# A decode block on one core: a head's wq and wo in two loads at two places of the turn instead of one

## The chip, the cores and the metric

The kernel runs on one core of one Trainium2 chip. The metric is the device time of one execution, in microseconds (us); lower is better. Three runs of the kernel before gave 1358.25 to 1359.9 us, median 1359.09. All data is float32.

## The reference, cut to what matters

One new token for each of B = 2 sequences goes through an attention block with a cache and then through a bilinear feed-forward block:

```python
q = (_layernorm(x) @ wq).reshape(B, 1, 16, 256)           # D = 448 -> 16 heads of 256
scores = einsum("bhqd,bhkd->bhqk", q, k_cache) * 256**-0.5 # 8192 keys per head and sequence
o = einsum("bhqk,bhkd->bhqd", softmax(scores), v_cache)
h = x + o.reshape(B, 1, 4096) @ wo
n = _layernorm(h)
h2 = h + ((n @ w_gate) * (n @ w_up)) @ w_down
```

`k_cache` and `v_cache` hold 2 x 16 x 8192 x 256 numbers each. All of both caches must be read once, together with the weights: 561 MB by the profile's count.

## The kernel before, in words

**Tiling.** One head and one sequence ("a query", b = 0 or 1) has 8192 keys. They come in NCH = 2 chunks of 4096 keys, each a tile of 128 partitions x 32 keys x 256 numbers, 4096 KB. There are two K buffers (`k_sb[0]`, `k_sb[1]`) and two V buffers (`v_sb[0]`, `v_sb[1]`), one for each chunk number. A load may start into a buffer only when the engine that reads its old contents is through with them.

**Engines.** VectorE (DVE) does the scores: for each half chunk a product (L222, `prod`) and a reduction (L225, `s_sb`), so four instructions for a chunk. TensorE (PE) mixes V with the softmax weights (`mix`, L252), projects the next head's query (`query`, L206 and L211, from `wq_sb`) and adds the head's part of the output projection (`mixed`, L270, from `wo_sb`). ScalarE (ACT) does the exponentials and small copies. SyncE (SP) issues every load, strictly in the order of the program: a load that has to wait holds up all loads behind it.

**The loop.** `For_i` over the 16 heads (L428) has three arms: the first head, the last head with the feed-forward behind it, and the fourteen heads between, all through `query_steps`. A turn works on b = 0 and then on b = 1 of its head. V runs one query behind K: while K of (head h, b = 0) is scored, V of (head h - 1, b = 1) is loaded and mixed, and with K of (h, 1) goes V of (h, 0). So `wo` of head h - 1 is first needed in the b = 0 part of turn h (L270, `if b == B - 1` of the previous query), and `wq` of head h + 1 in the b = 1 part of turn h, between the mixing of the two chunks of V (L295 to L298).

**The order of the loads.** A turn of the middle arm issues nine loads. In this text a and b stand for the turn's first and second query:

| load | K0a | V0a | W | K1a | V1a | K0b | V0b | K1b | V1b |
|---|---|---|---|---|---|---|---|---|---|
| KB | 4096 | 4096 | 896 | 4096 | 4096 | 4096 | 4096 | 4096 | 4096 |
| completion semaphore | 0 | 1 | 2 | 3 | 4 | 5 | 6 | 7 | 0 |

W is one load into the tile `w_sb`, whose first half is `wo` of head h - 1 and whose second half is `wq` of head h + 1 (L175, called at L284).

**The waits.** The framework that builds the program writes all waits itself. Its rule, read from the compiled program of the kernel before: every load adds to one of eight completion semaphores, given out in turn, 0 to 7 and then 0 again, starting at 0 in each arm; and a load is issued only when all earlier loads on its own semaphore have landed, those of the previous turn included. K0a, the first load of a turn, waits in that program for semaphore 0 (so for V1b of the turn before, the last load on it), for semaphore 5 (K0b of the turn before, which wrote the same buffer) and for DVE's last product on `k_sb[0]`. V0a waits for semaphores 1, 6 and 7 and for PE's `mix` of `v_sb[0]`. W waits for semaphore 2 and for PE's last `query` matmul of the turn before. V1a waits for semaphore 4 and for PE's whole previous turn. The first arm issues three loads in the loop, the last arm twenty-one, on the same eight semaphores from 0 on.

Of the kernel before, what the change touches and what calls it, by code (L numbers as in the profile page):

```python
# [8 lines left out]
F32 = mybir.dt.float32  # L9
# [4 lines left out]
B, D, H, SK, DH, F = 2, 448, 16, 8192, 256, 1792  # L14
EPS = 1e-5
P = 128
# [9 lines left out]
WQ, WO = 3 * DH + DH // 2, 2 * D  # L26
# [17 lines left out]
def tile_decode_block(  # L44
# [2 lines left out]
    x: bass.AP,  # L47
    k_cache: bass.AP,
    v_cache: bass.AP,
    w: bass.AP,  # L50
    wg: bass.AP,
    wu: bass.AP,
    wd: bass.AP,
# [12 lines left out]
    nc = tc.nc  # L66
    ctx.enter_context(tc.manual_schedule())
    const = ctx.enter_context(tc.tile_pool(name="const", bufs=1))
# [35 lines left out]

    k_sb = [const.tile([P, JC, DH], F32, name=f"k_sb{c}") for c in range(NCH)]
    v_sb = [const.tile([P, JC, DH], F32, name=f"v_sb{c}") for c in range(NCH)]
    w_sb = const.tile([P, WO + WQ], F32, name="w_sb")
    wo_sb, wq_sb = w_sb[:, :WO], w_sb[:, WO:]
    ff_sb = const.tile([P, NF * D], F32, name="ff_sb")
    q_sb = [const.tile([P, DH], F32, name=f"q_sb{b}") for b in range(B)]  # L110
    s_sb = [const.tile([P, NJ], F32, name=f"s_sb{b}") for b in range(B)]
# [52 lines left out]
    def load_cache(dst, src, bh, c, parts=(JC,)):  # L164
        n = P * JC
        keys = src.rearrange("b h s d -> (b h) s d")[bass.ds(bh, 1), c * n : (c + 1) * n]
        keys = keys.rearrange("o (p j) d -> p (o j) d", p=P)
        at = 0
        for k in parts:
            nc.sync.dma_start(dst[:, at : at + k, :], keys[:, at : at + k, :])  # L170
            at += k

    def load_w(h, lo=0, hi=WO + WQ):

        nc.sync.dma_start(w_sb[:, lo:hi], w[bass.ds(h, 1)].rearrange("o p n -> p (o n)")[:, lo:hi])  # L175

    load_w(H - 1, lo=WO)

    nc.vector.tensor_copy(x_sb[:, D:], x_sb[:, D - HALF : D])
    xT = transposed(x_sb, "x")  # L180
# [22 lines left out]
    def query(b):  # L203

        for c in range(DC - 1):
            nc.tensor.matmul(  # L206
                q_ps[b][:, :DH], xb[:, c, b, :], wq_sb[:, c * DH : (c + 1) * DH],
                start=(c == 0), stop=False,
            )
        for k in range(2):  # L210
            nc.tensor.matmul(  # L211
                q_ps[b][:, k * HD : (k + 1) * HD], xb[:, DC - 1 + k, b, :], wq_sb[:, 3 * DH :],
                start=False, stop=(k == 1),
            )

    def take_query(b):
        nc.scalar.activation(q_sb[b], q_ps[b][:, :DH], AF.Copy)  # L217

    def scores(b, part, at=k_sb):

        c, k = divmod(part, 2)
        nc.vector.tensor_mul(  # L222
            prod, at[c][:, k * HC : (k + 1) * HC, :], q_sb[b][:, None, :].to_broadcast([P, HC, DH])
        )
        nc.vector.tensor_reduce(  # L225
            s_sb[b][:, part * HC : (part + 1) * HC], prod, axis=AX.X, op=ALU.add
        )

    def top(b):

        nc.vector.tensor_reduce(m_sb, s_sb[b], axis=AX.X, op=ALU.max)  # L231
        nc.tensor.transpose(sm_ps[0][:1, :P], m_sb, ident)  # L232

    def softmax(b):
        nc.vector.tensor_reduce(nm_sb, sm_ps[0][:1, :P], axis=AX.X, op=ALU.max, negate=True)  # L235
        nb_ps = sm_ps[1][:, 0:1]
        nc.tensor.matmul(nb_ps, row, nm_sb, start=True, stop=True)  # L237
        nc.scalar.activation(nb_sb, nb_ps, AF.Copy)  # L238
        nc.scalar.activation(  # L239
            p_sb[b], s_sb[b], AF.Exp, bias=nb_sb, scale=DH**-0.5, accum_out=lsum_sb  # L240
        )
        nc.tensor.matmul(sm_ps[1][:, 1:2], ones, lsum_sb, start=True, stop=True)  # L242

    def norm():
        nc.vector.reciprocal(rl_sb, sm_ps[1][:, 1:2])

    def mix(b, c):

        for t in range(c * JC // 2, (c + 1) * JC // 2):
            j = 2 * t - c * JC  # L250
            g = 32 * (t % 4)
            nc.tensor.matmul(  # L252
                o_ps[b][g : g + 2, :], p_sb[b][:, 2 * t : 2 * t + 2], v_sb[c][:, j : j + 2, :],
                start=(t < 4), stop=(t >= NJ // 2 - 4),
            )

    def mixed(b, last=False):

        nc.scalar.activation(o_sb, o_ps[b], AF.Copy)  # L259
        oT_ps = sm_ps[1][:, 2:4]  # L260
        for c in range(2):
            for k in range(2):
                nc.tensor.matmul(  # L263
                    oT_ps[:, c : c + 1], o_sb[:, (2 * k + c) * P : (2 * k + c + 1) * P],
                    sel[:, k : k + 1], start=(k == 0), stop=(k == 1),
                )
        nc.scalar.activation(oT_sb[:, :, b], oT_ps, AF.Copy, scale=rl_sb)  # L267
        if b == B - 1:
            for c in range(2):
                nc.tensor.matmul(  # L270
                    acc_ps, oT_sb[:, c, :], wo_sb[:, c * D : (c + 1) * D],
                    start=False, stop=(last and c == 1),
                )

    def query_steps(h, first, more):

        for b in range(B):
            before = b > 0 or not first
            for c in range(NCH):
                if not first or (b > 0 and c > 0):  # L280
                    load_cache(k_sb[c], k_cache, b * H + h, c)
                    load_cache(v_sb[c], v_cache, h if b else H - 1 + h, c)
                if c == 0 and b == first:
                    load_w(h, WO if first else 0, WO + (WQ if more else 0))  # L284
            at = k_sb if before else k_first
            scores(b, 0, at)
            if before:
                softmax(1 - b)
            scores(b, 1, at)
            if before:  # L290
                norm()
            for part in range(2, 2 * NCH):
                scores(b, part, at)
            for c in range(NCH):
                if c > 0 and b == 1 and more:  # L295
                    query(0)
                    query(1)
                    take_query(0)  # L298
                if before:
                    mix(1 - b, c)  # L300
            if before:
                mixed(1 - b)
            top(b)
            if b == 1 and more:
                take_query(1)
# [8 lines left out]
    def attend_last():  # L314

        for c in range(NCH):
            load_cache(v_sb[c], v_cache, B * H - 1, c, LAST if c == NCH - 1 else (JC,))
        load_w(0, hi=WO)
        nc.sync.dma_start(wg_t, wg)
        softmax(1)  # L320
        norm()
        mix(1, 0)
        nc.sync.dma_start(wu_t, wu)
        mix(1, 1)

        at = 0
        for n in (8, 4, 2):
            nc.sync.dma_start(
                wd_t[:, at : at + n, :].rearrange("p n d -> p (n d)"), wd[:, at * D : (at + n) * D]
            )  # L330
            at += n
        mixed(1, last=True)
# [113 lines left out]
def pack(np, inputs):  # L446

    got = {n: np.ascontiguousarray(inputs[n]) for n in ("A_x", "A_k_cache", "A_v_cache")}
    wq, wo = np.asarray(inputs["A_wq"]), np.asarray(inputs["A_wo"])
    rows = []  # L450
    for h in range(H):
        a = wq[:, h * DH : (h + 1) * DH]
        top = a[: 3 * P].reshape(3, P, DH).transpose(1, 0, 2).reshape(P, 3 * DH)
        last = np.concatenate([a[3 * P :, :HD], a[3 * P :, HD:]], axis=0)
        rows.append(np.concatenate([top, last], axis=1))

    wo = wo.reshape(H, 2, P, D).transpose(0, 2, 1, 3).reshape(H, P, WO)
    got["w"] = np.concatenate([np.roll(wo, 1, axis=0), np.roll(np.stack(rows), -1, axis=0)], axis=2)
    for name in ("B_w_gate", "B_w_up"):
        a = np.asarray(inputs[name])  # L460
        top = a[: 3 * P].reshape(3, P, F).transpose(1, 0, 2).reshape(P, 3 * F)
        col = [a[3 * P :, FO[g] : FO[g] + FG[g]] for g in range(4)]
        last = np.concatenate(
            [np.concatenate([col[k], col[k + 2]], axis=1) for k in range(2)], axis=0
        )
        got[name] = np.concatenate([top, last], axis=1)
    a = np.asarray(inputs["B_w_down"]).reshape(NF, P, D)
    a = a[[FO[g] // P + n for n, g in FF]]
    got["wd"] = a.transpose(1, 0, 2).reshape(P, NF * D)
    return {k: np.ascontiguousarray(v) for k, v in got.items()}  # L470
# [25 lines left out]
```

## Time and profile before

| what | us |
|---|---|
| median of 3 runs | 1359.09 |
| the profiled execution: device time | 1357.73 |
| its span in the profile | 1355.9 |
| DVE busy | 1153.7 |
| PE busy | 554.5 |
| time in which DMA packets were under way, as a share of 16 engines' span (SP's queue) | 96.9% |

The profile page gives each engine's busy time, the mean DMA rate and the chain of work that ended last. Other views answer for a window of time: the timeline of one engine in order (start, duration, instruction, what it waited for), the busy times and the DMA rate of a stretch, the chain of work piece by piece, SP's own waits, and for a load the time from issue to landing. The times in these views count from the span's start, so the 1.8 us between the span and the device time lie around the span.

### The profile page before, as it was taken

How to read it: one execution, taken by the hardware profiler on the slowest of the kernel's cores; microseconds unless marked ns; L12 is line 12 of the kernel's file. 1: busy time of each engine (PE TensorE's matmuls, PEld its weight loads, DVE VectorE, ACT ScalarE, POOL GpSimd, SP SyncE). 2: the span in 40 equal slices, each digit the busy share in tenths (PEclk: the TensorE clock that was granted, in tenths of full speed). 3: DMA queues.
4: the chain of work that ended last, by engine and by line, in shares of the span. 5: the costliest groups of instructions: out<-in, count | busy, mean ns of one | idle time of the engine just before them, and what ended most of it. 6: DMA issues, size and time to landing. Idle time of an engine off the chain costs nothing.

```text
span 1355.9 us, 9160 instructions
## 1 busy us (share of the span) xinstructions
PE 554.5 (41%) x3094; PEld 194.1 (14%) x3094; DVE 1153.7 (85%) x395; ACT 61.7 (5%) x197; POOL 1.2 (0%) x8
## 2 busy tenths in 40 slices
PE   3224455252352633524334453434425245263347
PEld 2111111020020210201111021111102002021013
DVE  7999989798897988889898897988979889898871
ACT  1000000000000000000000000000000000000000
POOL 0000000000000000000000000000000000000000
PEclk7567766676775656768667566677767666576668
DMA  9999898999999999999999999999999999999998
GB/s 409 408 426 433 372 437 372 441 430 389 433 397 432 432 392 431 395 430 433 393 430 394 429 402 428 433 388 431 400 429 433 397 433 388 429 433 400 433 422 342
DMA packets 22213, 561.45 MB, mean 414 GB/s; under 512 B 2482, under 2 KB 2484, under 8 KB 5044
## 3 DMA queue, kind: packets, MB, share of 16 engines
q1 hardware_dynamic: 22184, 561.20, 96.9%
q8 instruction: 13, 0.21, 0.1%
q14 instruction: 4, 0.03, 0.0%
q10 hardware_dynamic: 12, 0.01, 0.0%
HBM read 561.19 MB, written 0.00 MB: 414 GB/s over the span
## 4 chain that ended last, share of the span: by engine, by line
DMA 59%; DVE 36%; PE 3%; issue 2%; DVEq 0%; ACT 0%; SPq 0%; ACTq 0%
DMA k_sb<-in_A_k_cache_dram 59%; DVE prod L222 23%; DVE s_sb L225 12%; PE o_ps L252 1%; PE q_ps L352 1%; PE sm_ps L156 0%; PE y_ps L411 0%; PE acc_ps L270 0%; PE q_ps L206 0%; DMA x_sb<-in_A_x_dram 0%; DVEq L222 0%; PE acc_ps L198 0%; PE sm_ps L135 0%; PE sm_ps L263 0%; SPq L170 0%
## 5 line engine op out<-in xcount | busy, mean ns | idle before, releaser
L222 DVE TENSOR_TENSOR prod<-k_sb,q_sb 128x4096 f32<-128x4096 f32 x126 | 556.9, 4420 | 156.0 <-DMA k_sb<-in_A_k_cache_dram 147.8
L225 DVE TENSOR_REDUCE s_sb<-prod 128x16 f32<-128x4096 f32 x128 | 565.8, 4420 | 5.4
L252 PE MATMUL o_ps<-v_sb,p_sb 128*2 128x512 f32 x2048 | 357.6, 862 | 335.0 <-DMA v_sb<-in_A_v_cache_dram 227.3
L237 PE MATMUL sm_ps<-nm_sb,row 1*128 1x1 f32 x64 | 17.9, 347 | 325.7 <-DVE nm_sb L235 312.5
L252 PEld LDWEIGHTS o_ps<-v_sb,p_sb 128*2 128x2 f32 x2048 | 58.6, 107 | 592.2 <-issue 457.5
L237 PEld LDWEIGHTS sm_ps<-nm_sb,row 1*128 1x128 f32 x64 | 15.7, 302 | 332.8 <-issue 197.8
L206 PE MATMUL q_ps<-w_sb,xb 128*128 128x256 f32 x192 | 50.2, 399 | 0.0
L259 ACT ACTIVATE o_sb<-o_ps 128x512 f32<-128x512 f32 x32 | 19.1, 597 | 641.3 <-PE o_ps L252 641.3
L263 PE MATMUL sm_ps<-sel,o_sb 128*128 128x1 f32 x256 | 33.7, 253 | 25.7 <-ACT o_sb L259 25.7
L270 PE MATMUL acc_ps<-w_sb,oT_sb 128*2 128x448 f32 x64 | 38.2, 736 | 5.6 <-ACT oT_sb L267 5.6
L232 PE MATMUL sm_ps<-ident,m_sb 128*1 128x128 f32 x32 | 10.1, 314 | 73.2 <-DVE m_sb L231 73.2
L263 PEld LDWEIGHTS sm_ps<-sel,o_sb 128*128 128x128 f32 x256 | 31.0, 191 | 56.4 <-ACT o_sb L259 56.4
L206 PEld LDWEIGHTS q_ps<-w_sb,xb 128*128 128x128 f32 x192 | 35.1, 197 | 18.6 <-issue 14.9
L242 PE MATMUL sm_ps<-lsum_sb,ones 128*128 128x1 f32 x64 | 18.7, 361 | 25.3 <-ACT p_sb L239 25.3
L238 ACT ACTIVATE nb_sb<-sm_ps 128x1 f32<-128x1 f32 x32 | 5.5, 171 | 449.8 <-PE sm_ps L237 449.8
L211 PEld LDWEIGHTS q_ps<-w_sb,xb 128*128 128x128 f32 x128 | 19.8, 196 | 1.8
L242 PEld LDWEIGHTS sm_ps<-lsum_sb,ones 128*128 128x128 f32 x64 | 16.0, 309 | 28.1 <-ACT p_sb L239 28.1
L211 PE MATMUL q_ps<-w_sb,xb 128*128 128x128 f32 x128 | 19.9, 279 | 0.0
L217 ACT ACTIVATE q_sb<-q_ps 128x256 f32<-128x256 f32 x32 | 12.2, 380 | 134.7 <-PE q_ps L211 129.1
L232 PEld LDWEIGHTS sm_ps<-ident,m_sb 128*1 128x1 f32 x32 | 2.5, 79 | 92.1 <-issue 60.0
L362 DVE COPY h_sb<-acc_ps 2x448 f32<-2x448 f32 x1 | 0.6, 612 | 14.4 <-PE acc_ps L270 14.4
L239 ACT ACTIVATE p_sb<-s_sb,nb_sb 128x64 f32<-128x64 f32 x32 | 11.1, 348 | 1.0
(78 smaller groups left out, 95.7 us busy)
## 6 DMA issues: line engine op xcount, KB each, us to landing
v_sb<-in_A_v_cache_dram SPq DMA_DIRECT2D x63, 4096.0 KB, 32.7
k_sb<-in_A_k_cache_dram SPq DMA_DIRECT2D x62, 4096.0 KB, 25.3
w_sb<-in_w_dram SPq DMA_DIRECT2D x14, 896.0 KB, 22.7
k_sb<-in_A_k_cache_dram SPq DMA_DIRECT2D x2, 2048.0 KB, 10.0
v_sb<-in_A_k_cache_dram SPq DMA_DIRECT2D x1, 4096.0 KB, 20.9
ff_sb<-in_B_w_gate_dram SPq DMA_DIRECT2D x1, 3136.0 KB, 22.2
v_sb<-in_B_w_up_dram SPq DMA_DIRECT2D x1, 3136.0 KB, 18.5
v_sb<-in_A_v_cache_dram SPq DMA_DIRECT2D x1, 2048.0 KB, 11.2
```

Of the source, the lines that this page charges most:

```text
L206: nc.tensor.matmul(q_ps[b][:, :DH], xb[:, c, b, :], wq_sb[:, c * DH : (c + 1) * DH], start=(c == 0), stop=False,)
L211: nc.tensor.matmul(q_ps[b][:, k * HD : (k + 1) * HD], xb[:, DC - 1 + k, b, :], wq_sb[:, 3 * DH :], start=False, stop=(k == 1),)
L222: nc.vector.tensor_mul(prod, at[c][:, k * HC : (k + 1) * HC, :], q_sb[b][:, None, :].to_broadcast([P, HC, DH]))
L225: nc.vector.tensor_reduce(s_sb[b][:, part * HC : (part + 1) * HC], prod, axis=AX.X, op=ALU.add)
L232: nc.tensor.transpose(sm_ps[0][:1, :P], m_sb, ident)
L237: nc.tensor.matmul(nb_ps, row, nm_sb, start=True, stop=True)
L242: nc.tensor.matmul(sm_ps[1][:, 1:2], ones, lsum_sb, start=True, stop=True)
L252: nc.tensor.matmul(o_ps[b][g : g + 2, :], p_sb[b][:, 2 * t : 2 * t + 2], v_sb[c][:, j : j + 2, :], start=(t < 4), stop=(t >= NJ // 2 - 4),)
L259: nc.scalar.activation(o_sb, o_ps[b], AF.Copy)
L263: nc.tensor.matmul(oT_ps[:, c : c + 1], o_sb[:, (2 * k + c) * P : (2 * k + c + 1) * P], sel[:, k : k + 1], start=(k == 0), stop=(k == 1),)
L270: nc.tensor.matmul(acc_ps, oT_sb[:, c, :], wo_sb[:, c * D : (c + 1) * D], start=False, stop=(last and c == 1),)
L352: nc.tensor.matmul(ps[32 * g : 32 * g + 32, : end - lo], xs.rearrange("p b r -> p (b r)"), w[:, at + lo : at + end], start=(c == 0), stop= ...
```

## The change

`w_sb` becomes two tiles, `wq_sb` and `wo_sb`, and the packed input `w` two inputs, `wq` and `wo`. In a turn of the middle arm `wo` (448 KB) is issued where W was, behind V0a, and `wq` (448 KB) behind V0b. The first arm still issues one load of `wq`, the last arm one of `wo` in `query_steps` and one in `attend_last`, at the same places as before.

```diff
-    w_sb = const.tile([P, WO + WQ], F32, name="w_sb")
-    wo_sb, wq_sb = w_sb[:, :WO], w_sb[:, WO:]
+    wq_sb = const.tile([P, WQ], F32, name="wq_sb")
+    wo_sb = const.tile([P, WO], F32, name="wo_sb")
...
-    def load_w(h, lo=0, hi=WO + WQ):
-
-        nc.sync.dma_start(w_sb[:, lo:hi], w[bass.ds(h, 1)].rearrange("o p n -> p (o n)")[:, lo:hi])
-
-    load_w(H - 1, lo=WO)
+    def load_w(dst, src, h):
+        nc.sync.dma_start(dst, src[bass.ds(h, 1)].rearrange("o p n -> p (o n)"))
+
+    load_w(wq_sb, wq, H - 1)
...
                 if not first or (b > 0 and c > 0):
                     load_cache(k_sb[c], k_cache, b * H + h, c)
                     load_cache(v_sb[c], v_cache, h if b else H - 1 + h, c)
-                if c == 0 and b == first:
-                    load_w(h, WO if first else 0, WO + (WQ if more else 0))
+                if c == 0 and b == 0 and before:
+                    load_w(wo_sb, wo, h)
+                if c == 0 and b == 1 and more:
+                    load_w(wq_sb, wq, h)
...
-        load_w(0, hi=WO)
+        load_w(wo_sb, wo, 0)
...
+    got["wq"] = np.roll(np.stack(rows), -1, axis=0)
     wo = wo.reshape(H, 2, P, D).transpose(0, 2, 1, 3).reshape(H, P, WO)
-    got["w"] = np.concatenate([np.roll(wo, 1, axis=0), np.roll(np.stack(rows), -1, axis=0)], axis=2)
+    got["wo"] = np.roll(wo, 1, axis=0)
```

More of the change, by code (lines that the diff above doesn't have):

```diff
@@ L49, in tile_decode_block @@
     v_cache: bass.AP,
-    w: bass.AP,
+    wq: bass.AP,
+    wo: bass.AP,
     wg: bass.AP,
```

## The prediction

> **What bounds the kernel now.** I read the page first: span, busy times, DMA queues, chain.
>
> ```profile
> span 1355.9 us, 9160 instructions
> ...
> PE 554.5 (41%) x3094; PEld 194.1 (14%) x3094; DVE 1153.7 (85%) x395; ACT 61.7 (5%) x197; POOL 1.2 (0%) x8
> ...
> q1 hardware_dynamic: 22184, 561.20, 96.9%
> ...
> HBM read 561.19 MB, written 0.00 MB: 414 GB/s over the span
> ...
> DMA 59%; DVE 36%; PE 3%; issue 2%; DVEq 0%; ACT 0%; SPq 0%; ACTq 0%
> ```
>
> DVE, the busiest engine, has 202 us free; the DMA queue has 3%. So I asked how fast the stream of loads can go and where it does not. Two windows of one turn, cut where DVE starts on K1a, on K1b and on the next turn's K1a (columns: us, PE, PEld, DVE, ACT and POOL busy, PE clock, DMA share, GB/s), then single us around the turn's end:
>
> ```profile
> 679.77:718.60 38.83, 17.61 (x100) 7.12 (x101) 35.77 (x11) 1.85 (x6) 0.00 (x0) 0.70 1.00 432
> 718.60:762.66 44.06, 15.28 (x81) 4.18 (x79) 35.76 (x11) 1.75 (x6) 0.00 (x0) 0.63 0.95 402
> ...
> 726.00:727.00 1.00, 0.00 (x0) 0.00 (x0) 1.00 (x1) 0.00 (x0) 0.00 (x0) 0.50 1.22 524
> 727.00:728.00 1.00, 0.00 (x0) 0.00 (x0) 0.96 (x2) 0.00 (x0) 0.00 (x0) 0.50 0.01 0
> 728.00:729.00 1.00, 0.74 (x4) 0.11 (x8) 1.00 (x1) 0.00 (x0) 0.00 (x0) 0.50 0.00 0
> 729.00:730.00 1.00, 1.00 (x12) 0.22 (x8) 1.00 (x1) 0.00 (x0) 0.00 (x0) 0.50 1.32 360
> ```
>
> The first half moves four loads without a hole, at 432 GB/s: 38.83 / 4 = 9.71 us a load. The second has a hole of two us in which nothing moves. SP's timeline and the loads' times to landing say why:
>
> ```profile
> 671.61 0.33 SPq L170 DMA_DIRECT2D k_sb<-in_A_k_cache_dram  x1
> 674.47 0.33 SPq L170 DMA_DIRECT2D v_sb<-in_A_v_cache_dram  x1
> 693.21 0.33 SPq L170 DMA_DIRECT2D k_sb<-in_A_k_cache_dram  x1
> 694.83 0.33 SPq L170 DMA_DIRECT2D v_sb<-in_A_v_cache_dram  x1
> 728.61 0.33 SPq L170 DMA_DIRECT2D k_sb<-in_A_k_cache_dram  x1
> 729.36 0.33 SPq L170 DMA_DIRECT2D v_sb<-in_A_v_cache_dram  x1
> 730.03 0.33 SPq L175 DMA_DIRECT2D w_sb<-in_w_dram  x1
> 732.14 0.33 SPq L170 DMA_DIRECT2D k_sb<-in_A_k_cache_dram  x1
> 737.10 0.33 SPq L170 DMA_DIRECT2D v_sb<-in_A_v_cache_dram  x1
> ```
> ```profile
> v_sb<-in_A_v_cache_dram SPq DMA_DIRECT2D x1, 4096.0 KB, 33.4
> ```
> ```profile
> k_sb<-in_A_k_cache_dram SPq DMA_DIRECT2D x1, 4096.0 KB, 12.3
> ```
> ```profile
> SPq L492 <- SPq L492: 407.7, 14, 32.4
> ```
>
> V1b, issued at 694.83, lands 33.4 later, at 728.2. K0a of the next turn is issued 0.4 us after that and lands 12.3 later, at 740.9. SP stood still from 695.2 to 728.6; SP's waits show 14 such stops at the turn's end (L492), as many as there are turns that follow a turn of the middle arm (1 to 2 up to 14 to 15). The landing of V1b is what K0a waits for: both lie on completion semaphore 0. The buffer is no reason, as DVE shows:
>
> ```profile
> 708.17 4.40 DVE L222 TENSOR_TENSOR prod<-k_sb,q_sb 128x4096 f32<-128x4096 f32 x1
> ...
> 718.60 4.42 DVE L222 TENSOR_TENSOR prod<-k_sb,q_sb 128x4096 f32<-128x4096 f32 x1 [1.50 <-DMA k_sb<-in_A_k_cache_dram]
> ```
>
> The last product on `k_sb[0]` ends at 712.6, 16 us before K0a goes out. So at each of 14 turn ends the queue runs empty.
>
> **What the hole costs.** From the chain piece by piece: its first piece of a load, and then K1a of turn 3 and of turn 15, 12 turns apart (columns: start, us):
>
> ```profile
> 118.65 18.70 DMA k_sb<-in_A_k_cache_dram
> ...
> 235.38 30.30 DMA k_sb<-in_A_k_cache_dram
> ...
> 1229.01 28.97 DMA k_sb<-in_A_k_cache_dram
> ```
>
> A turn takes (1229.01 - 235.38) / 12 = 82.80 us. Without a hole it would take 2 x 38.83 for eight cache loads and 896 / 16384 x 38.83 = 2.12 for W: 79.78. The hole costs 3.02 us. At the one boundary above: 0.4 + 12.3 - 9.71 = 3.0. Two of these 3 us show as no packet at all; the third is the new load's start. From one boundary to the next (640 to 735 us) the shortest of eleven loads landed 12.0 us after issue; it can only be the K0a of 646, which starts in an empty queue, and makes that hole 2.7:
>
> ```profile
> DMA to landing us min/median/max: 12.0/23.3/34.3
> ```
>
> **The change part by part.** *Semaphores.* Ten loads, given out by the same rule: K0a 0, V0a 1, wo 2, K1a 3, V1a 4, K0b 5, V0b 6, wq 7, K1b 0, V1b 1. K0a now waits for K1b, the last but one. In the turn above K1b landed when DVE began on it, 718.6; K0a could go out at about 719 (its buffer has been free since 712.6), 9.7 us earlier, with V1b still moving until 728. V0a is held by semaphore 1 for V1b's landing, so it goes out at about 729, as now; behind it in SP's queue stand wo and K1a. But by then K0a moves, until 728.2 + 9.7 = 737.9: the queue holds 9 us of work where it was empty. K1a waits for DVE's second product on K1b (732, as now), V1a for PE's end of the turn (737, as now); the queue then holds V0a and wo until 748.7. From there K loads go out at the pace of DVE, each a load or more ahead. So the hole goes, 3.02 us a turn. If the cover of 9 us were gone (K1b not landed long before V1b), the hole would be back whole; nothing in the order of the loads does that.
>
> *wq.* It is issued right behind V0b, as W is behind V0a (0.7 us later in the timeline). Its semaphore (7, wq of the turn before) and PE's last use of `wq_sb` lie a turn back, so it waits for nothing. It must have landed when PE projects:
>
> ```profile
> 710.19 5.08 PE L252 MATMUL o_ps<-v_sb,p_sb 128*2 128x512 f32 x32
> 715.19 1.56 PE L206 MATMUL q_ps<-w_sb,xb 128*128 128x256 f32 x6
> ...
> 718.33 0.61 PE L211 MATMUL q_ps<-w_sb,xb 128*128 128x128 f32 x4
> ```
>
> V0b lands first, then wq about 1.05 us later; PE mixes V0b for 5 us before it reads wq. That covers it with 4 us. Were it gone, each us of lateness would move the projection, which ends at 719 now and whose result DVE needs when the next K0a has landed (738): 19 us more until it costs anything.
>
> *wo.* It is in its old place, half as long, and no longer waits for the projection of the turn before, which ends at 719, 10 us before wo goes out. Nothing.
>
> *One load more per turn.* Three loads of the feed-forward weights queue behind one another at the end, 1792, 896 and 448 KB:
>
> ```profile
> 1326.79 0.33 SPq L328 DMA_DIRECT2D v_sb<-in_wd_dram  x1
> ...
> 1327.65 0.33 SPq L328 DMA_DIRECT2D v_sb<-in_wd_dram  x1
> ```
> ```profile
> L328 SPq DMA_DIRECT2D v_sb<-in_wd_dram x1: 327/327/327, 1328.5 to 1328.5; - x1
> ```
> ```profile
> v_sb<-in_wd_dram SPq DMA_DIRECT2D x1, 1792.0 KB, 21.0
> v_sb<-in_wd_dram SPq DMA_DIRECT2D x1, 896.0 KB, 22.3
> v_sb<-in_wd_dram SPq DMA_DIRECT2D x1, 448.0 KB, 22.5
> ```
>
> They land at 1347.8, 1349.95 and 1351.0: 896 KB took 2.15, 448 KB 1.05 us. Two of 448 KB take 2.1 to 2.3 with the rounding, against 2.12 to 2.15 for one of 896: between -0.05 and +0.2 us, and I take +0.1. The other bound, far off, is a load alone, wq ahead of the loop, landing 3.3 us after issue:
>
> ```profile
> w_sb<-in_w_dram SPq DMA_DIRECT2D x1, 448.0 KB, 3.3
> ```
>
> That is 3.3 - 1.05 = 2.25 us beyond its bytes. The rows at the end are the nearer: same size, same queue, other loads ahead. The Trainium skill speaks against this part: "DMA: Bandwidth & Descriptors", section "Rules for kernel authors", asks for 1 MiB or more in a DMA, and its section "Anatomy of one DMA — SWDGE (gpsimd) path" fits about 2.0 us plus the bytes for each; as an estimate from that page the extra load would cost 14 x 2.0 = 28 us. The three landings, 1.05 us for a whole load of 448 KB, do not show such a fixed part between queued loads.
>
> *What is late next.* The new turn is 79.78 + 0.1 = 79.9 us; DVE has 35.77 + 35.76 = 71.5 of it busy, so the stream stays the bound.
>
> **The sum.** 14 x (3.02 - 0.1) = 40.9 us off. The first turns (DVE-bound: the chain has no load before 118.65 us) and the end behind the last K load keep their length. From the profiled execution's 1357.7: 1316.8. It lies 1.4 below the median of the runs, so for a median: 1318.2, which I give as 1318. Check: 561.2 MB at 432 GB/s are 1299 us, which leaves 19 for start and end.
>
> **The rivals.**
> 1. *A fixed price for the extra load*, its lone latency of 2.25 us: 14 x (3.02 - 2.25) = 10.8 off, 1347 to 1348. For it: the 3.3 us row. Against it: the landings at the end. 0.04. The Trainium skill's rule on small DMAs, named above, would give about this.
> 2. *The wait does not move*: the framework gives the semaphores out otherwise than I read, or K0a waits for V1b by another dependence. Then 1359. Against it: the compiled program names only semaphores 0 and 5 and DVE for K0a. 0.06.
> 3. *Slower: the wait stays and the extra load has its fixed price.* Place: in the stream between V0b and K1b; price up to 2.25 us a turn; 14 x 2.25 = 31.5, 1391. It decides from 0.2 us a load on, if the hole stays; if the hole goes, it would need over 3.0. 0.03.
>
> **How the numbers follow.** The forecast has 0.87. Its own spread: the hole 2.7 (the shorter one above) to 3.1 us (3.02 and the rounding of its rows), the load -0.05 to +0.2, the offset to the median 0 to 1.4: from 1357.7 - 14 x 3.15 = 1314 to 1357.7 - 14 x 2.5 + 1.4 = 1324. The far price of the load, 2.25 us, makes rival 1 and is not in this spread. I take 1312 to 1326, a little on each side for the spread of runs. The rivals' 0.13 lie outside. A measurement here tells about 0.2% (2.7 us) from no change: faster 0.91 (forecast and rival 1), same 0.06, slower 0.03.
>
> **What would show it.** K0a issued some 0.4 us after K1b's landing, SP's stop at the turn's end 24 us instead of 33, followed by a second stop of 9 to 10 at V0a; no us at 0 GB/s at a turn's end; a turn of 79.9 in the chain; some 426 GB/s over the span; PE with no wait for wq. Wrong, if K0a still follows V1b, if a new hole opens between K0a and V0a, or if the half turn with wq takes over 40 us for its 38.83 + 1.06.

## The result and the profile after

| | before | changed |
|---|---|---|
| median of 6 runs, us | 1359.48 | 1316.78 |
| the profiled execution, us | 1357.73 | 1316.87 |
| its span, us | 1355.9 | 1315.0 |

The ratio is 0.9687, with a 95% interval of 0.9675 to 0.9700: 3.1% faster. The page of the changed kernel, the lines that answer to those shown of before:

```profile
span 1315.0 us, 9215 instructions
...
PE 548.1 (42%) x3094; PEld 192.3 (15%) x3094; DVE 1153.7 (88%) x395; ACT 61.7 (5%) x197; POOL 1.3 (0%) x8
...
q1 hardware_dynamic: 24200, 561.20, 99.5%
...
HBM read 561.19 MB, written 0.00 MB: 427 GB/s over the span
```

The same bytes, the same DVE time and the same PE instructions lie in 41 us less, and the DMA queue is busy 99.5% of the span instead of 96.9%. SP's timeline at the turn's end, and the landing times of the loads issued at 672.17 (K1b), 673.52 (V1b) and 698.99 (the next K0a):

```profile
672.17 0.33 SPq L171 DMA_DIRECT2D k_sb<-in_A_k_cache_dram  x1
673.52 0.33 SPq L171 DMA_DIRECT2D v_sb<-in_A_v_cache_dram  x1
698.99 0.33 SPq L171 DMA_DIRECT2D k_sb<-in_A_k_cache_dram  x1
708.69 0.33 SPq L171 DMA_DIRECT2D v_sb<-in_A_v_cache_dram  x1
709.29 0.33 SPq L175 DMA_DIRECT2D wo_sb<-in_wo_dram  x1
712.23 0.33 SPq L171 DMA_DIRECT2D k_sb<-in_A_k_cache_dram  x1
```
```profile
k_sb<-in_A_k_cache_dram SPq DMA_DIRECT2D x1, 4096.0 KB, 26.4
v_sb<-in_A_v_cache_dram SPq DMA_DIRECT2D x1, 4096.0 KB, 34.8
```
```profile
k_sb<-in_A_k_cache_dram SPq DMA_DIRECT2D x1, 4096.0 KB, 19.0
```

K1b lands at 672.17 + 26.4 = 698.6, and K0a goes out 0.4 us later. V1b lands at 673.52 + 34.8 = 708.3, and V0a goes out 0.4 us after that. K0a takes 19.0 us to land instead of 12.3, and yet it is early: it lies behind V1b in a queue that still moves, and lands 718.0 - 708.3 = 9.7 us after V1b, which is one load's time. Before, it landed 12.7 us after V1b. SP's waits show the first stop shorter, at most 24.0 us instead of 32.4, and behind it a second one, which waits for V1b: 27 stops in all instead of 14 (L495 stands where L492 stood before):

```profile
SPq L495 <- SPq L495: 413.3, 27, 24.0
```

The windows (us, PE, PEld, DVE, ACT and POOL busy, PE clock, DMA share, GB/s), a long one and the two us in which V1b lands:

```profile
160.00:1160.00 1000.00, 419.16 (x2217) 139.95 (x2217) 896.24 (x276) 44.72 (x149) 0.00 (x0) 0.67 1.00 431
```
```profile
708.00:709.00 1.00, 0.65 (x4) 0.11 (x8) 1.00 (x1) 0.00 (x0) 0.00 (x0) 0.50 0.84 360
709.00:710.00 1.00, 1.00 (x8) 0.15 (x4) 1.00 (x1) 0.00 (x0) 0.00 (x0) 0.50 1.06 459
```

Where before two us at 0 GB/s stood, the stream of loads now runs on, and over 1000 us it keeps 431 GB/s, the rate that the first half of a turn had before (432). SP issues K1a of turn 3 and of turn 15 here:

```profile
232.42 0.33 SPq L171 DMA_DIRECT2D k_sb<-in_A_k_cache_dram  x1
```
```profile
1192.05 0.33 SPq L171 DMA_DIRECT2D k_sb<-in_A_k_cache_dram  x1
```

A turn takes (1192.05 - 232.42) / 12 = 79.97 us, against 82.80.

### The profile page after: what moved, and what is told of

It is laid out like the page before. It is cut to its first block, busy times and chain, and to the rows that moved or that the text cites. A ratio compares the mean times of both kernels' runs of the same rounds, so it can differ in the third digit from the quotient of the medians.

```text
span 1315.0 us, 9215 instructions
## 1 busy us (share of the span) xinstructions
PE 548.1 (42%) x3094; PEld 192.3 (15%) x3094; DVE 1153.7 (88%) x395; ACT 61.7 (5%) x197; POOL 1.3 (0%) x8
## 3 DMA queue, kind: packets, MB, share of 16 engines
q1 hardware_dynamic: 24200, 561.20, 99.5%
## 5 line engine op out<-in xcount | busy, mean ns | idle before, releaser
L206 PE MATMUL q_ps<-wq_sb,xb 128*128 128x256 f32 x192 | 49.7, 396 | 0.0
L206 PEld LDWEIGHTS q_ps<-wq_sb,xb 128*128 128x128 f32 x192 | 34.7, 194 | 18.5 <-issue 15.0
L270 PE MATMUL acc_ps<-wo_sb,oT_sb 128*2 128x448 f32 x64 | 34.5, 673 | 5.6 <-ACT oT_sb L267 5.6
L211 PEld LDWEIGHTS q_ps<-wq_sb,xb 128*128 128x128 f32 x128 | 19.7, 194 | 1.8
L211 PE MATMUL q_ps<-wq_sb,xb 128*128 128x128 f32 x128 | 19.6, 276 | 0.0
## 6 DMA issues: line engine op xcount, KB each, us to landing
k_sb<-in_A_k_cache_dram SPq DMA_DIRECT2D x62, 4096.0 KB, 26.4
```

The costliest lines, as they stand in the source:

```text
L206: nc.tensor.matmul(q_ps[b][:, :DH], xb[:, c, b, :], wq_sb[:, c * DH : (c + 1) * DH], start=(c == 0), stop=False,)
L211: nc.tensor.matmul(q_ps[b][:, k * HD : (k + 1) * HD], xb[:, DC - 1 + k, b, :], wq_sb[:, 3 * DH :], start=False, stop=(k == 1),)
L270: nc.tensor.matmul(acc_ps, oT_sb[:, c, :], wo_sb[:, c * D : (c + 1) * D], start=False, stop=(last and c == 1),)
```

## The experiments

The theory: K0a waits for the last load that used its completion semaphore; with nine loads that is V1b, the very last load, and the queue runs empty; with ten it is K1b. Rival A: the gain comes from the place of wq, which evens out the two halves of a turn. Rival B: it comes from the order of waits, since no load stands behind one that waits for the last turn's projection. Ratios are to the kernel before in the same session.

| kernel | loads in a turn | K0a shares a semaphore with | median us | ratio (95%) |
|---|---|---|---|---|
| extra_load | 10 | K1b | 1318.64 | 0.9710 (0.9693 to 0.9726) |
| old_place | 10 | K1b | 1317.01 | 0.9700 (0.9684 to 0.9716) |
| w_behind_v0b | 9 | V1b | 1357.71 | 0.9994 (0.9985 to 1.0004) |
| loads17 | 17 | V1b | 1365.23 | 1.0057 (1.0040 to 1.0074) |
| loads18 | 18 | K1b | 1325.62 | 0.9762 (0.9746 to 0.9778) |
| spare_last | 10 | V1b (64 KB behind it) | 1358.46 | 1.0003 (0.9993 to 1.0013) |
| v1b_28_4 | 10 | 7/8 of V1b (512 KB behind) | 1341.82 | 0.9877 (0.9860 to 0.9893) |
| v1b_16_16 | 10 | half of V1b (2048 KB behind) | 1318.19 | 0.9704 (0.9688 to 0.9720) |
| loads11 | 11 | wq | 1318.39 | 0.9709 (0.9696 to 0.9723) |
| wg_early | 10 | K1b | 1321.23 | 0.9732 (0.9718 to 0.9745) |

**extra_load**: the kernel before and one load that nobody needs.

```diff
+    spare = const.tile([P, P], F32, name="spare")
...
                     load_w(h, WO if first else 0, WO + (WQ if more else 0))
+                if c == 0 and b == 1 and more and not first:
+                    nc.sync.dma_start(spare, w[bass.ds(h, 1)].rearrange("o p n -> p (o n)")[:, :P])
```

> The kernel before with W whole and in its old place, and one more load of 64 KB behind V0b into a tile that nobody reads; ten loads a turn. Theory (the number of loads decides, since K0a waits for the last load that used its semaphore): the hole of 3.0 us goes in 14 turns, and the spare load costs its bytes, 0.15 us, and 0.1 to 0.2 more: 1359.5 - 14 x 2.7 = 1321 to 1322. Rival A (the gain is that wq moved to the other half turn) and rival B (the gain is that no load waits for the projection of the turn before): 1359.5 + 14 x 0.3 = 1364.

Measured 1318.64. Its SP timeline, from the spare load to the next turn's K0a:

```profile
655.66 0.33 SPq L287 DMA_DIRECT2D spare<-in_w_dram  x1
673.34 0.33 SPq L171 DMA_DIRECT2D k_sb<-in_A_k_cache_dram  x1
675.35 0.33 SPq L171 DMA_DIRECT2D v_sb<-in_A_v_cache_dram  x1
699.26 0.33 SPq L171 DMA_DIRECT2D k_sb<-in_A_k_cache_dram  x1
```

Behind V1b SP stops for 23.6 us instead of 33.4. More work on the busiest resource makes the kernel 2.9% faster: with W whole, in its old place and with its old wait, so neither rival is needed. The median lies 2 to 3 us below what was expected. 1.3 us of that is the session, in which the kernel before ran at 1358.23 and not at 1359.5; what made the rest is open.

**old_place**: the changed kernel, both loads where W was.

```diff
-                if c == 0 and b == 0 and before:
-                    load_w(wo_sb, wo, h)
-                if c == 0 and b == 1 and more:
-                    load_w(wq_sb, wq, h)
+                if c == 0 and b == first:
+                    if not first:
+                        load_w(wo_sb, wo, h)
+                    if more:
+                        load_w(wq_sb, wq, h)
```

> The changed kernel with wq loaded right behind wo, where W was; ten loads a turn, wq waits for the projection again. Theory: K0a still waits for K1b only, 1317. Rival A (place): 1359. Rival B (the wait for the projection): 1359.

Measured 1317.01, as the changed kernel. The new place of wq gives nothing that can be measured.

**w_behind_v0b**: the place alone, with nine loads.

```diff
-                if c == 0 and b == first:
-                    load_w(h, WO if first else 0, WO + (WQ if more else 0))
+                if c == 0 and b == 1 and more:
+                    load_w(h)
...
-        load_w(0, hi=WO)
+        load_w(H - 1, hi=WO)
...
-    got["w"] = np.concatenate([np.roll(wo, 1, axis=0), np.roll(
+    got["w"] = np.concatenate([wo, np.roll(
```

> W whole, with wo of this head instead of the last one, behind V0b; nine loads a turn, none of which waits for the projection of the turn before. Theory: V1b and K0a share a semaphore again, the hole stays, 1359 to 1360. Rivals A and B: 1316.

Measured 1357.71, no change. SP's waits and the windows at a turn's end:

```profile
SPq L492 <- SPq L492: 368.9, 14, 29.6
```
```profile
728.00:729.00 1.00, 0.00 (x0) 0.00 (x0) 1.00 (x1) 0.00 (x0) 0.00 (x0) 0.50 0.08 33
729.00:730.00 1.00, 0.18 (x4) 0.11 (x8) 0.97 (x2) 0.00 (x0) 0.00 (x0) 0.50 0.00 0
730.00:731.00 1.00, 1.00 (x8) 0.15 (x4) 1.00 (x1) 0.00 (x0) 0.00 (x0) 0.50 0.00 0
```

The hole is there, 14 stops again. Rival A expected 1316 and falls: the load has moved to the other half of the turn, and nothing is won. For rival B this kernel is a weaker test than it was meant to be. No load waits for the last turn's projection any more, but W now brings `wo` of this head and has to wait for this turn's output projection, which still reads `w_sb`; K1b stands behind it:

```profile
SPq L175 <- PE acc_ps L270: 294.1, 14, 24.4
```

Rival B falls by extra_load, where W has its old wait and the gain is there all the same, and by SP's waits of the kernel before, which put only 2 stops down to the last turn's projection, 12.3 us in all:

```profile
SPq L175 <- PE q_ps L211: 12.3, 2, 9.4
```

**loads17 and loads18**: the changed kernel with wo and wq in more pieces in the middle turns. Seventeen loads bring V1b back onto K0a's semaphore (17 = 2 x 8 + 1), eighteen do not.

```diff
-    def load_w(dst, src, h):
-        nc.sync.dma_start(dst, src[bass.ds(h, 1)].rearrange("o p n -> p (o n)"))
+    def load_w(dst, src, h, parts=(WO,)):
+        at = 0
+        for n in parts:
+            rows = src[bass.ds(h, 1)].rearrange("o p n -> p (o n)")
+            nc.sync.dma_start(dst[:, at : at + n], rows[:, at : at + n])
+            at += n
...
+                mid = more and not first
                 if c == 0 and b == 0 and before:
-                    load_w(wo_sb, wo, h)
+                    load_w(wo_sb, wo, h, (224,) * 4 if mid else (WO,))
                 if c == 0 and b == 1 and more:
-                    load_w(wq_sb, wq, h)
+                    load_w(wq_sb, wq, h, (192,) * 4 + (128,) if mid else (WQ,))
```

(In loads18 wo has the parts of wq.)

> The changed kernel with wo in four and wq in five loads in the middle turns, places as in the changed kernel; seventeen loads a turn, so that V1b shares K0a's semaphore as it does with nine. Theory: the hole is back, and seven more loads cost 0.1 to 0.2 us each: 1359.5 + 14 x 8 x 0.1 to 0.2 = 1371 to 1382. Rivals A and B: no hole, 1317 + 14 x 7 x 0.1 to 0.2 = 1327 to 1336.

> The changed kernel with wo and wq in five loads each in the middle turns; eighteen loads a turn, so that K1b, not V1b, shares K0a's semaphore, as with ten. Theory: no hole, and eight more loads at the price that the seventeen loads showed, (1365.2 - 1358.2) / (14 x 8) = 0.06 us: 1316.8 + 14 x 8 x 0.06 = 1324. If seventeen was slow for its many small loads and not for the semaphore: 1365 or more.

Measured 1365.23 and 1325.62. One load more takes 40 us off. The turn's end of loads17, and the long window of loads18:

```profile
730.00:731.00 1.00, 0.00 (x0) 0.00 (x0) 1.00 (x1) 0.00 (x0) 0.00 (x0) 0.50 0.31 131
731.00:732.00 1.00, 0.15 (x4) 0.11 (x8) 0.97 (x2) 0.00 (x0) 0.00 (x0) 0.50 0.01 0
732.00:733.00 1.00, 1.00 (x8) 0.15 (x4) 1.00 (x1) 0.00 (x0) 0.00 (x0) 0.50 0.35 98
```
```profile
160.00:1160.00 1000.00, 418.04 (x2200) 138.45 (x2204) 889.81 (x274) 43.83 (x147) 0.00 (x0) 0.66 1.01 428
```

So it is the count modulo eight that brings the hole, and not the number or the size of the loads. The pair also prices a load: loads17 stands 7.0 us above the kernel before with 14 x 8 loads more, 0.06 us each; loads18 8.8 us above the changed kernel (which ran in another session), 0.08 us each. The length of a turn, from K1a of turn 3 to K1a of turn 15, says the same: 83.25 us in loads17 against 82.80, and 80.58 in loads18 against 79.97, so 0.06 and 0.08 us for each of eight loads. The expectation of loads17, 1371 to 1382, was too high mainly for that reason: it took 0.1 to 0.2.

**spare_last**: the spare load of 64 KB behind V1b instead of behind V0b.

```diff
+                if c == 1 and b == 1 and more and not first:
+                    nc.sync.dma_start(spare, w[bass.ds(h, 1)].rearrange("o p n -> p (o n)")[:, :P])
```

> The kernel before with one more load of 64 KB, behind V1b, the last of the turn; ten loads a turn, K0a shares V1b's semaphore, V0a that of the spare load. Theory (what counts is how much is still to move behind the load that K0a waits for, and here it is 0.15 us): the hole stays 3.0 - 0.15, the spare load costs 0.15 + 0.06: 1358.2 + 14 x 0.06 = 1359. If the number ten by itself were enough: 1318.6, as with the spare load behind V0b.

Measured 1358.46. SP's waits show the old stops:

```profile
SPq L495 <- SPq L495: 401.8, 14, 32.1
```

Ten loads are not enough. K0a again waits for V1b, and 64 KB behind it cover nothing.

**v1b_28_4 and v1b_16_16**: the kernel before, V1b in two loads; 512 or 2048 KB lie behind the part that K0a waits for.

```diff
-                    load_cache(v_sb[c], v_cache, h if b else H - 1 + h, c)
+                    end = b == 1 and c == 1 and more and not first
+                    load_cache(v_sb[c], v_cache, h if b else H - 1 + h, c, (28, 4) if end else (JC,))
```

> The kernel before with V1b in two loads, 3584 and 512 KB; ten loads a turn, K0a shares the semaphore of the first part, and the second, 512 KB or 1.21 us, is still to move. Theory: 1.21 us of the hole of 3.02 are covered, less 0.06 for the load: 1358.2 - 14 x 1.15 = 1342. If any cover closes the whole hole: 1317.

> The same with two parts of 2048 KB; behind the first 4.85 us are still to move. Theory: more than the hole of 3.02, so all of it goes: 1358.2 - 14 x (3.02 - 0.06) = 1317. If the cover needed were a whole load (9.7 us): half the gain, 1337.

Measured 1341.82 and 1318.19. In SP's timeline of the first, V1b's two loads, K0a and V0a:

```profile
688.48 0.88 SPq L170 DMA_DIRECT2D v_sb<-in_A_v_cache_dram  x2
...
720.41 0.33 SPq L170 DMA_DIRECT2D k_sb<-in_A_k_cache_dram  x1
721.66 0.33 SPq L170 DMA_DIRECT2D v_sb<-in_A_v_cache_dram  x1
```

K0a follows the first part and V0a the second, 1.25 us later, where before they were 0.75 apart. 512 KB, 1.21 us of the stream, bring (1358.44 - 1341.82) / 14 = 1.19 us a turn; 2048 KB bring (1358.44 - 1318.19) / 14 = 2.88, as much as a whole load does. As far as these two points show, the hole is closed us for us by what is still to move when K0a goes out, and more than the hole's 3 us is of no use. Where between 512 and 2048 KB the gain stops was not measured.

**loads11**: wo in two loads of 448 columns; the lead is one load longer.

```diff
-                    load_w(wo_sb, wo, h)
+                    load_w(wo_sb, wo, h, (448, 448) if mid else (WO,))
```

> The changed kernel with wo in two loads in the middle turns; eleven loads a turn, K0a shares wq's semaphore, V0a that of K1b, the first part of wo that of V1b, so SP may run one load further ahead. Theory: the stream was already whole, so nothing more is won and one load costs 0.06 us a turn: 1316.8 + 14 x 0.06 = 1317.6. If the shorter lead still lets some of the stream's time go: 1315 or less.

Measured 1318.39, so nothing more is to be had by a longer lead.

**wg_early**, a miss: an attempt on the 2 us that the stream still loses in the first turns.

```diff
+                if c == 1 and b == 1 and first:
+                    nc.sync.dma_start(wg_t, wg)
...
         load_w(wo_sb, wo, 0)
-        nc.sync.dma_start(wg_t, wg)
         softmax(1)
```

> The changed kernel with the load of w_gate (3136 KB, a tile of its own) in the first turn behind V1b, where the stream still has gaps, instead of at the end. Between 60 and 67 us of the changed kernel the rate is 324 and 279 GB/s against 431: 1.2 + 0.7 = 2 us are free there. Theory (every us of the stream's idle time is a us of the kernel): 1316.8 - 2 = 1315. If the end hides the load of w_gate anyway: 1316.8.

Measured 1321.23, 4.4 us above the changed kernel's median. The two ran in different sessions, but the intervals of their ratios, 0.9718 to 0.9745 and 0.9675 to 0.9700, do not touch. The first window below is of the changed kernel, the second of wg_early:

```profile
60.00:67.00 7.00, 7.00 (x41) 2.64 (x42) 6.96 (x2) 0.00 (x0) 0.00 (x0) 0.75 0.81 311
```
```profile
60.00:67.00 7.00, 7.00 (x39) 2.09 (x39) 6.96 (x2) 0.00 (x0) 0.00 (x0) 0.67 1.01 429
```

The gap is filled, as meant. But the last K load of the kernel goes out later (SP's timelines, changed kernel and wg_early):

```profile
1232.02 0.33 SPq L171 DMA_DIRECT2D k_sb<-in_A_k_cache_dram  x1
```
```profile
1237.46 0.33 SPq L171 DMA_DIRECT2D k_sb<-in_A_k_cache_dram  x1
```

5.4 us: the 7.4 us of w_gate (3136 KB at 431 GB/s) less the 2 us filled. What stands behind that K load shifts with it, and the end wins back only part: from that load's issue to the end of the span it is 82.98 us in the changed kernel and 80.54 in wg_early. In both chains PE's last wait for V ends, at 1286.7 and at 1292.1; from there the chain of the changed kernel goes by the landing of w_down, that of wg_early by PE's own work to its last matmuls:

```profile
1273.20 13.45 DMA v_sb<-in_A_v_cache_dram
...
1287.75 22.50 DMA v_sb<-in_wd_dram
```
```profile
1278.22 13.90 DMA v_sb<-in_A_v_cache_dram
...
1310.87 2.92 PE y_ps L414 x112
```

Both theories of this run fall. At the end the work behind the last V load is nearly as long as the loads left over, so most of w_gate stood in its shadow: taking 7.4 us of loads away shortens the end by 2.4. None of these kernels is faster than the changed one.

## Why the prediction was right

- *The bound.* Right. The span is the stream's, and no engine's: with the hole gone the DMA share of the long window is 1.00 and DVE's busy time has not moved. The range, 1312 to 1326, held 1316.78.
- *K0a waits for V1b because of the shared semaphore.* Right, and shown by loads17 against loads18, spare_last and w_behind_v0b: nine or seventeen loads, or ten with a small one at the end, leave the hole; ten, eleven and eighteen with a whole load behind take it away. That K0a waits for a landing, and for which one, shows in v1b_28_4, where it follows the first part of V1b.
- *Ten loads let K0a go out with V1b still moving, and V0a with K0a.* Right to the tenth: 0.4 us behind K1b's landing, a second stop at V0a, the first stop 24.0 us.
- *The hole costs 3.02 us a turn.* Right. The direct evidence is v1b_28_4 and v1b_16_16, where 1.21 us of cover bring 1.19 and more than enough brings 2.88. Only two of the three us show as no packet. The third lies in the new load's start, as the prediction had it: the two us behind the empty ones moved 360 and 164 GB/s instead of 432, which is 0.8 us lost. The first of them is the last window that the prediction shows, the second this one of the kernel before:

```profile
730.00:731.00 1.00, 1.00 (x12) 0.22 (x8) 1.00 (x1) 0.00 (x0) 0.00 (x0) 0.50 0.51 164
```

- *wq lands in time.* Right. In the changed kernel V0b and wq are issued at 655.38 and 655.98 and land so:

```profile
v_sb<-in_A_v_cache_dram SPq DMA_DIRECT2D x1, 4096.0 KB, 32.4
wq_sb<-in_wq_dram SPq DMA_DIRECT2D x1, 448.0 KB, 32.9
```
```profile
L206 PE MATMUL q_ps<-wq_sb,xb x12: 379/379/483, 695.6 to 698.5; 128*128 128x256 f32 x12
```

  wq is there at 688.9, 1.1 us behind V0b, and PE reads it from 695.6 on: 6.7 us of cover, where 4 were forecast.
- *The extra load costs +0.1 us.* Within its bounds, -0.05 to +0.2. The changed turn, 79.97 us, is 0.19 longer than the 79.78 worked out without a hole, and the slightly lower rate of 431 GB/s is in that too; the smaller loads of loads17 and loads18 cost 0.06 to 0.08 each. The Trainium skill's fixed price of about 2.0 us for a DMA, in "DMA: Bandwidth & Descriptors", section "Anatomy of one DMA — SWDGE (gpsimd) path", which the page gives for the path through GpSimd, is not what a load issued by SP costs here between others of the queue: 112 of them cost 7.0 to 8.8 us, where an estimate from the page would be 224. A lone load does show something near it (3.3 us for 448 KB, 2.25 beyond its bytes), and so does K0a before, which starts into the empty queue (12.3 us, 2.6 beyond the 9.71 of a load in the stream).
- *The sum.* 40.9 us off the profiled execution's 1357.73 were forecast, and 40.86 were measured on the profiled ones. Thirteen holes are 1229.01 - 1192.05 = 37.0 us at K1a of turn 15, 2.84 each (3.02 less the 0.19 above). The fourteenth, at the start of that turn, does not move K1a's issue, which waits for DVE, but what comes behind: the last K load goes out at 1232.02 instead of 1271.54, 39.5 us earlier, and DVE begins on it at 1257.43 instead of 1298.20, 40.8 us earlier. From there both kernels take the same 57.6 to 57.7 us to the end, as the prediction had it. So 14 holes gave 39.5 us, and 1.3 us more were won while the last K load was on its way; by what is open, and that the sum holds to a tenth is partly luck. The 1.4 us added for the median were of no use: the changed kernel's profiled execution lies on its median. One reading of the prediction is not exact and changes nothing: the chain does have a load before 118.65 us, that of x, 2.1 us at the very start.
- *The rivals.* A fixed price of 2.25 us for a load (rival 1) and with it rival 3 fall by loads17 and loads18; rival 2, that the wait stays, by the timeline.

## What to carry to other kernels

Where a framework gives DMA completions out over a few semaphores and, as this one, lets a load wait for the earlier loads on its own semaphore even if its buffer is long free, count the loads of a loop's turn modulo the number of semaphores, and see that the first load of a turn does not share one with the last load of the turn before. The sign in a profile is a queue at 0 GB/s once a turn while the buffer's last reader ended long ago, and the issuing engine standing until a landing. To close such a hole, enough must still be to move when the next load goes out: 512 KB were too little here and 2048 KB enough, and the hole's own length, 3 us or 1.3 MB at 431 GB/s, is an estimate of what it takes. How the loads are then split matters little, at 0.06 to 0.08 us for each further one.

## What the runs showed that was not expected

A load that nobody reads, 64 KB in each of 14 turns, took 40 us off a kernel bound by its loads. A load between others cost 0.06 to 0.08 us beyond its bytes down to 64 KB (128 partitions of 512 bytes), far below what a lone load takes. And a transfer of 7.4 us moved from the end of the kernel into a gap of 2 us at the beginning made it some 4 us slower, since the end got only 2.4 us shorter by it.
